# Sliding-window attention followed by a gated network: the first weight block is consumed by contraction halves, the third tile's output also takes seven products, and the order of the work is drawn up anew

## The chip, the cores and the metric

The kernel runs on one core of a Trainium2 chip. A core has a matrix engine (PE, whose weight loads are listed as PEld), a vector engine (DVE), a scalar engine (ACT), a general engine (POOL, which here also issues the loads from DRAM) and a synchronising engine (SP, which here issues the stores). PE multiplies a stationary block by a moving block and writes to one of eight accumulator banks of 128 partitions by 512 floats. The metric is the device time of one execution in microseconds (us).

## The reference

Attention over 8 batches, 8 heads, 576 positions and head size 64, where a position sees itself and the 63 before it; the result, as 4608 rows of 512, goes through a gated network of inner width 1536.

```python
scores = scale * np.matmul(q, k.transpose(0, 1, 3, 2))
rel = pos[:, None] - pos[None, :]
mask = (rel >= 0) & (rel < 64)
attn = softmax(np.where(mask, scores, -1e9))
x = (attn @ v).transpose(0, 2, 1, 3).reshape(4608, 512)
out = (np.maximum(x @ w_gate, 0.0) * (x @ w_val)) @ w_out
```

Inputs and output are float32 in DRAM; the kernel computes in 16-bit floats with float32 accumulation.

## The kernel before

**Tiles.** The 4608 rows are nine tiles of 512 rows, numbered 0 to 8. A tile is eight windows of 64 positions. For each tile the kernel computes scores (L377, L385), exponentials (ACT, L645), the product with v (L391), a reciprocal and a scaling into `xw` (DVE, L660 and L398), and a transpose into the stationary layout `xt` (DVE, `turn`, L403). Then come the two hidden products with the gate and the value weights, the rectifier and their product into `g_sb`, and the output product with `wo`.

**Two ways to multiply.** Tile 0's hidden layer is direct (`direct_block`, PE at L750, rectifier on ACT at L760, product on DVE at L762). The hidden layers of tiles 1 to 8 (`fast_hidden`, PE at L842) form the two-by-two block product by seven block products in place of eight: sums of weight blocks (`us`, `vs`, formed once at L791), sums of x blocks (L716), and sums of results (DVE, L858). The output is direct for the tiles below `TF` (`output`, PE at L916: 12 groups of four 512-column products for each tile) and by seven products from tile `TF` on (`fast_output`, PE at L1005: 14 groups of six 256-column products, four sums of `g_sb` blocks on DVE at L973, three sums of results on DVE at L1041). The latter needs sums of blocks of `wo` (`w_sums`, L950), one of which is written over `wo` itself, and so only after the last direct output.

**The start.** `first_part` is written out by hand. Tile 0's first six windows are two units of 192 rows (u = 0 and 1), each in two head halves (hh = 0 and 1) of 256 of the 512 columns of x. The list of steps is: 93 small products of zeros on PE (`PADS`, L424), loads of the first q, k and v, the first four of 12 column blocks of the gate weight `wg` and then of the value weight `wv`, each in two halves a = 0 and 1 of the contraction (`w_part`, L337), scores and values of both units, and for each unit and head half a `recip`, a `norm` and a `turn`. Products of zeros (`keep_hot`, L453, three times, and L502 into bank 7) lie between the steps on PE. The half a = 0 of the contraction is head half 0 of x, and a = 1 is head half 1.

**The rest.** `second_part` lists every other step as an `Op` with a key, an expected duration on each engine that can do it, the steps that it comes after, and the accumulator banks and buffers that it takes and gives back. `Plan.run` walks through expected time when the program is built. For each engine it takes the ready step with the lowest key, and it emits the steps in that order. So the order on each engine's queue is fixed by the keys, which come from the table `K` (one value for a kind of step, and a correction for each tile under `K["d"]`), by the expected durations, and by the times at which engines, banks and transfers are expected to be free after the first part. Loads are issued by POOL, in the order of their keys, between its arithmetic. `Plan.fetch` models the arrival of PE's own instructions; `Plan.fill` counts products into long waits, though `emit` leaves those out of the program.

**Tile 0, first two units.** `direct_block` is called for u = 0 and 1 and for two pairs of the first four 128-wide column blocks. Each call does, for each column block, the four contraction steps of one weight in a row:

```python
for b, f in enumerate(fs):
    for c in range(NC):
        nc.tensor.matmul(bank[i][:, b * n:b * n + n], wt[:, c, f * 128:f * 128 + 128],
                         xs[0][:, c, c0:c0 + n], start=(c == 0), stop=(c == NC - 1))
```

Of the kernel before, what the change touches and what calls it, by code (L numbers as in the profile page):

```python
# [12 lines left out]
ACT = mybir.ActivationFunctionType  # L13
MUL = mybir.AluOpType.mult
ADD = mybir.AluOpType.add
SUB = mybir.AluOpType.subtract
MAX = mybir.AluOpType.max
ONE_ONE = struct.unpack("<f", struct.pack("<I", 0x3C003C00))[0]


K = {"T1": 33.417, "STEP": 29.94, "wo1": 24.303, "wo2": 136.509, "q0": 0.81, "q1": 2.61, "q10": -9.561, "q11": 1.093, "v": -0.6, "v1": 1.142, "ql": 1.41, "qt": 0.88, "qti": 4.69, "vl": 0.91, "vc": 0.04, "vm": 1.83, "e": 7.62, "gap": 3.77, "gap1": -1.003, "r": -6.21, "tn": 1.66, "xf": 4.78, "wf": -1.338, "wfj": 2.6, "sn": 2.67, "su": -2.15, "re": 17.5, "mu": -6.61, "la": -4.79, "o0": 11.594, "o0j": 20.432, "o0s": -4.369, "oo": 0.007, "os": 0.386, "oj": 4.81, "gs": -1.18, "fo": 0.015, "fi": 0.098, "fs": 4.74, "fu": 0.27, "W0": 129.92, "TF": 3, "rs": 7.037, "rv": 3.751, "rt": 4.292, "wl": 1.63, "wln": 5.389, "l0": 0.003, "l1": 4.021, "lv": 1.186, "lvs": 12.368, "wo0": 25.921, "db": -7.955, "di": 1.563, "dv": 0.646, "slack": 0.3, "d2": 3.05, "bl": 9.0, "lv0": 18.364, "d": {'0:q0': 0.808, '0:fs': 1.88, '0:la': 1.692, '1:oo': 0.058, '0:fi': 0.024, '1:qt': 3.036, '1:os': -0.226, '0:vc': -1.15, '0:tn': -0.981, '0:qt': 0.904, '0:e': -2.629, '0:sn': 0.475, '0:vm': 0.58, '0:vl': 0.514, '0:ql': 0.128, '0:fu': -2.028, '1:tn': 3.174, '0:re': 0.858, '1:ql': -1.577, '0:xf': -0.14, '0:su': 0.053, '0:gap': 0.391, '0:r': -2.955, '0:oo': -0.042, '0:os': 0.025, '1:vm': 0.483, '1:fo': -0.017, '0:q1': 0.357, '1:sn': 0.632, '0:oj': -0.104, '0:qti': -0.947, '0:gs': -0.096, '0:fo': -0.029, '2:xf': -3.116, '1:oj': -0.851, '1:fu': -1.619, '1:gs': -1.956, '1:vl': 3.671, '1:fs': -1.692, '1:q0': -0.44, '1:re': 17.838, '1:qti': -0.251, '2:vl': -1.63, '1:xf': 0.54, '2:v': 0.897, '2:e': 3.091, '1:vc': -0.626, '2:gap': 1.519, '1:mu': -1.202, '2:oj': 1.272, '2:os': -0.152, '1:gap': -2.068, '1:su': 1.664, '1:q1': 0.09, '1:la': -0.927, '2:fu': -0.861, '2:q0': -1.678, '2:su': -3.121, '1:v': 0.703, '1:r': 0.099, '2:tn': 0.263, '2:mu': -0.767, '2:qti': -1.435, '2:sn': 0.235, '2:qt': 0.357, '3:re': -0.971, '3:su': 1.85, '2:gs': 0.316, '2:vc': -0.222, '2:fi': 0.018, '3:fs': 2.376, '2:oo': -0.024, '3:gs': -0.499, '2:ql': 2.087, '2:re': 1.781, '2:vm': -0.346, '2:la': -0.408, '3:fo': 0.105, '3:qt': -1.251, '3:qti': -0.756, '3:fi': 0.003, '3:r': 4.605, '4:tn': 4.441, '4:fo': 0.176, '3:sn': 1.86, '3:v': -0.191, '3:gap': 0.067, '3:q1': -1.861, '4:v': -2.381, '3:fu': -1.0, '3:e': -2.398, '3:ql': 0.244, '3:q0': -0.417, '4:ql': 1.859, '4:qti': -0.846, '3:oo': 0.017, '3:oj': -1.455, '3:mu': 5.549, '3:vl': -0.094, '3:la': -1.756, '3:os': 0.07, '4:qt': -2.162, '5:v': 2.345, '5:e': -6.12, '5:gap': -0.396, '4:re': 16.126, '4:r': -3.179, '4:os': 0.054, '4:q0': -0.903, '4:gap': -1.023, '4:fu': -1.144, '5:vm': 1.185, '4:fi': -0.029, '4:vm': 1.023, '4:la': 2.23, '4:vl': 0.037, '5:tn': -1.009, '5:r': -1.653, '5:fu': 0.073, '5:re': 3.794, '4:q1': 1.992, '4:sn': 1.164, '4:xf': -1.831, '5:fi': -0.019, '4:mu': 1.169, '4:oj': 1.089, '5:qti': -1.537, '5:fo': -0.021, '5:xf': -1.396, '5:gs': -0.82, '5:mu': -2.334, '5:vc': -0.566, '5:oo': 0.002, '5:q0': -0.047, '4:vc': 0.378, '5:qt': -1.506, '4:fs': 0.072, '5:ql': -0.361, '5:oj': 0.91, '5:fs': -0.532, '5:q1': -0.028, '4:oo': -0.002, '5:la': 0.275, '6:oo': -0.051, '6:vl': -1.345, '6:v': 0.087, '7:vc': 2.102, '6:os': 0.034, '7:fo': -0.026, '6:tn': -1.475, '6:gap': -1.442, '6:xf': 3.27, '6:fi': -0.035, '6:fo': -0.054, '6:fu': -0.179, '6:qt': 0.741, '7:tn': -0.289, '7:vl': -0.177, '6:ql': -0.604, '7:re': 9.431, '7:fi': 0.019, '7:xf': -0.992, '6:vc': -0.932, '7:sn': -0.018, '6:e': 6.905, '6:q1': 1.236, '7:ql': -0.482, '7:e': -4.862, '7:qt': 1.66, '6:mu': -0.73, '7:gap': 0.823, '6:oj': 0.303, '6:q0': 0.231, '6:r': 2.887, '7:su': 1.478, '7:gs': -0.403, '7:q0': -0.079, '7:q1': -0.303, '7:vm': -1.095, '6:gs': -0.02, '7:mu': -0.49, '7:fs': 1.309, '7:la': -0.048, '7:os': 0.117, '7:qti': -1.407, '7:r': -0.97, '7:fu': -0.866, '6:re': 0.021, '6:la': 0.896, '7:oo': -0.007, '6:sn': 0.915}}


PLANS = []


class Op:
# [16 lines left out]
class Plan:  # L44
# [70 lines left out]
    def fill(self, o, t, emit):  # L115
        if t - self.free["PE"] < 0.7:
            return
# [1006 lines left out]
```

## Time and profile before

| what | value |
|---|---|
| median of 3 runs | 308.0 us (307.89 to 308.69) |
| profiled execution, its own time | 309.13 us |
| span of the profiled execution | 307.2 us |
| DVE, ACT, POOL busy | 246.2, 213.0, 229.8 us |
| transfers on the loads' queue | 18.29 MB as written, 51.1% of 16 engines' span |
| hidden layers of tiles 1 to 8, PE L842 | 1344 products of 128x256 |
| direct outputs of tiles 0, 1, 2, PE L916 | 144 products of 128x512 |
| seven-product outputs of tiles 3 to 8, PE L1005 | 504 products of 128x256 in the program |

The span runs from the first to the last recorded instruction; the 1.93 us between it and the execution's own time lie around it. PE's busy time is from modelled ends: a 128x256 product is shown as 273 ns long though the next starts 109 ns later, so short pauses between products do not show as idle. A row of the timeline has start, duration, engine, line and operation, tiles, shapes, the number of instructions merged into it, and in brackets how long the engine sat idle before the first of them and what ended that. A row of windows has, for a stretch, its length, each engine's busy time in it with the number of instructions, PE's granted clock, the mean busy share of the 16 transfer engines (over 1 where packets overlap) and the rate in GB/s.

### The profile page before, as it was taken

Reading aid. Unit: us, or ns where it says so; the run is one execution under the profiler, and the core shown is the slowest. Engines: PE = TensorE matmul, PEld = TensorE weight load, DVE = VectorE, ACT = ScalarE, POOL = GpSimd, SP = SyncE. Lnnn points to the kernel's source line nnn. Section 1 sums busy time; section 2 is a strip of 40 time slices with the busy share of each in tenths; the row PEclk is TensorE's granted clock in tenths of the full one; section 3 lists DMA queues with packets and bytes.
Section 4 is the critical chain, followed back from the end, with each engine's and each line's share of the span. In section 5 each row is a group of like instructions: output and inputs, shape, how many; then the busy total and the mean of one; then the engine's idle time right before and its main releaser. Section 6 shows DMA issues by size and latency. Waiting matters only on the chain.

```text
span 307.2 us, 11254 instructions
## 1 busy us (share of the span) xinstructions
PE 297.1 (97%) x4772; PEld 240.2 (78%) x4772; DVE 246.2 (80%) x422; ACT 213.0 (69%) x414; POOL 229.8 (75%) x233
## 2 busy tenths in 40 slices
PE   7889999998999999999999999999999999999995
PEld 5475845786757886777888888888888888888884
DVE  5858997988963997887989988878896789595762
ACT  4445335897768787788778786778687886878721
POOL 8696957998999899999189954995479157938520
PEclk9999999999999999999999999999999999999999
DMA  7999999983249953996694194674112011201033
GB/s 219 187 190 206 196 194 198 202 169 22 19 78 150 183 99 75 139 182 136 123 72 82 34 165 120 48 166 37 54 36 69 6 38 37 68 0 36 1 121 120
DMA packets 59074, 32.87 MB, mean 107 GB/s; under 512 B 39440, under 2 KB 53392, under 8 KB 59024
## 3 DMA queue, kind: packets, MB, share of 16 engines
q0 software_dynamic: 46672, 18.29, 51.1%
q1 hardware_dynamic: 12208, 13.80, 14.2%
q8 instruction: 37, 0.61, 0.8%
q14 instruction: 13, 0.11, 0.1%
q10 hardware_dynamic: 144, 0.07, 0.1%
HBM read 37.75 MB, written 9.44 MB: 154 GB/s over the span
## 4 chain that ended last, share of the span: by engine, by line
PE 85%; DMA 8%; POOL 3%; issue 2%; DVE 1%; ACT 0%; ACTq 0%; DVEq 0%; POOLq 0%
PE bank L842 48%; PE bank L1005 18%; PE bank L916 8%; PE bank L391 4%; PE bank L750 3%; DMA wo<-in_moe_w_out_dram 3%; DMA wv<-in_moe_w_val_dram 3%; DMA k<-in_k_dram 2%; PE bank L385 2%; PE bank L377 1%; POOL vs L791 1%; POOL v L356 1%; POOL q L347 0%; POOL k L347 0%; DVE xw L398 0%
## 5 line engine op out<-in xcount | busy, mean ns | idle before, releaser
L876 POOL TENSOR_TENSOR g_sb<-pr,pr 128x512 f16<-128x512 f32 x96 | 121.6, 1283 | 47.7 <-ACT pr L889 16.5
L858 DVE TENSOR_TENSOR pr<-bank,pr 128x512 f32<-128x512 f32 x144 | 92.6, 678 | 24.7 <-PE bank L842 21.9
L851 ACT COPY pr<-bank 128x512 f32<-128x512 f32 x144 | 79.9, 590 | 30.2 <-PE bank L842 27.9
L842 PE MATMUL bank<-xt,vs 128*128 128x256 f16 x384 | 56.7, 273 | 0.0
L842 PE MATMUL bank<-xt,us 128*128 128x256 f16 x384 | 56.2, 273 | 0.0
L867 ACT ACTIVATE pr<-pr 128x512 f32<-128x512 f32 x72 | 45.4, 639 | 5.9 <-DVE pr L858 5.5
L842 PE MATMUL bank<-xt,wg 128*128 128x256 f16 x288 | 42.8, 273 | 0.0
L842 PE MATMUL bank<-xt,wv 128*128 128x256 f16 x288 | 42.7, 273 | 0.0
L842 PEld LDWEIGHTS <-us 128*128 128x128 f16 x384 | 37.0, 98 | 6.5 <-issue 0.2
L842 PEld LDWEIGHTS <-vs 128*128 128x128 f16 x384 | 37.2, 98 | 4.7
L645 ACT ACTIVATE p<-bank 128x512 f16<-128x512 f32 (+1 forms) x68 | 35.7, 592 | 6.7 <-PE bank L385 6.5
L916 PE MATMUL bank<-wo,g_sb 128*128 128x512 f16 x144 | 35.9, 380 | 0.3 <-DMA wo<-in_moe_w_out_dram 0.3
L356 POOL DMA_DIRECT2D v<-in_v_dram x40 | 34.9, 883 | 0.5 <-issue 0.5
L889 ACT ACTIVATE pr<-bank 128x512 f32<-128x512 f32 x48 | 27.1, 601 | 6.7 <-PE bank L842 5.0
L842 PEld LDWEIGHTS <-wg 128*128 128x128 f16 x288 | 27.7, 98 | 4.7
L842 PEld LDWEIGHTS <-wv 128*128 128x128 f16 x288 | 28.1, 98 | 4.2
L1005 PEld LDWEIGHTS <-g_sb 128*128 128x128 f16 x288 | 27.9, 98 | 3.4
L1005 PE MATMUL bank<-wo,g_sb 128*128 128x256 f16 x216 | 28.4, 273 | 0.0
L398 DVE TENSOR_TENSOR xw<-bank,r 128x448 f16<-128x448 f32 (+2 forms) x45 | 25.8, 575 | 1.5
L403 DVE STREAM_TRANSPOSE xt<-xw 128x512 f16<-128x512 f16 (+2 forms) x38 | 25.0, 668 | 0.5 <-ACT xw L506 0.3
L1005 PEld LDWEIGHTS <-ss 128*128 128x128 f16 x216 | 21.0, 98 | 2.5
L916 PEld LDWEIGHTS <-g_sb 128*128 128x128 f16 x144 | 13.5, 98 | 11.3 <-issue 0.3
(95 smaller groups left out, 389.4 us busy)
## 6 DMA issues: line engine op xcount, KB each, us to landing
out_dram<-pr SPq DMA_DIRECT2D x35, 256.0 KB, 2.4
k<-in_k_dram POOLq DMA_DIRECT2D x15, 288.0 KB, 7.5
q<-in_q_dram POOLq DMA_DIRECT2D x15, 288.0 KB, 7.1
v<-in_v_dram POOLq DMA_DIRECT2D x32, 128.0 KB, 6.4
v<-v SPq DMA_DIRECT2D x12, 132.0 KB, 2.6
v<-v SPq DMA_DIRECT2D x24, 66.0 KB, 2.3
wg<-in_moe_w_gate_dram POOLq DMA_DIRECT2D x6, 256.0 KB, 6.6
wv<-in_moe_w_val_dram POOLq DMA_DIRECT2D x6, 256.0 KB, 7.9
```

Of the source, the lines that this page charges most:

```text
L356: nc.gpsimd.dma_start(v16s[b % 2][lo:hi, g, :, 0:64], v[b, :, 64 * g - 64 + lo:64 * g - 64 + hi].rearrange("h p d -> p h d"))
L398: nc.vector.tensor_tensor(x, blocks_of(to, n)[:, :, 0:D].rearrange("p s (c e) -> p s e c", e=2), r[:, :, :, None].to_broadcast([128, n, 2, ...
L403: nc.vector.transpose(xt[:, 2 * hh:2 * hh + 2, c0:c0 + n].rearrange("p e (s c) -> p s e c", c=32), x)
L645: nc.scalar.activation(pp[g][:, 0:n].rearrange("p n c -> p (n c)"), st[g][:, 0:64 * n], ACT.Exp, scale=scale)
L842: nc.tensor.matmul(slot[to][:, HT * m:HT * m + HT], w[:, kk, 128 * m:128 * m + 128], x[:, kk], start=(first and m == 0 and kk == 0), stop= ...
L851: lambda e, hold=hold, slot=slot: nc.scalar.copy(hold["x"], slot["A"]),
L858: nc.vector.tensor_tensor(hold["x"], slot[to], hold["x"], ADD)
L867: lambda e: nc.scalar.activation(hold["x"], hold["x"], ACT.Relu), after=[o])
L876: lambda e: VEC[e].tensor_tensor(gh[:, fs:fs + 2, h], pair(a["x"]), pair(b["x"]), MUL),
L889: lambda e, hold=hold, slot=slot, i=i: nc.scalar.activation(hold["x"], slot["A"], ACT.Copy if i else ACT.Relu),
L916: nc.tensor.matmul(bank["b"][:, 0:c1 - c0], gs[t % 2][:, f, 128 * sub:128 * sub + 128], wo[:, f, c0:c1], start=(j == 0 and i == 0), stop=( ...
L1005: nc.tensor.matmul(bank[to][:, HD * m:HD * m + HD], a[:, f, 128 * m:128 * m + 128], b[:, f], start=(first and m == 0 and f == 0), stop=(f ...
```

## The change

In the first part: the loads of the first weight block go in the order gate a = 0, value a = 0, gate a = 1, value a = 1; before it was both of gate, then both of value. The second unit's values follow the first unit's directly on PE; a `keep_hot` and the product of zeros into bank 7 between them are gone, and 78 small products of zeros stand at the start in place of 93. On DVE, head half 0 of unit 0 is turned right after its own `norm`; head half 1 of unit 0 is turned after its `norm` and both of unit 1's reciprocals.

In tile 0's first two units, `direct_halves` takes the place of `direct_block`. Each weight's work on a pair of column blocks is two steps, one for each half of the contraction, and a list `SEQ` of (unit, gate or value, half) gives the order of the eight; each waits for its own half of x and of the weight. `mark` tells the plan at what time these halves are expected.

In the table: `TF` is 2 in place of 3, so that tile 2's output is formed by seven products and the sums of `wo` come after tile 1's direct output. All other keys are new, with corrections for tile 8 too; `fill` is gone, and a constant in the model of instruction arrival is 4.8 where 6.5 stood. Among the keys are those of the weight loads: `wl` is -2.164 (1.63), `wln` 11.938 (5.389), `wo0`, `wo1`, `wo2` are 23.517, 27.481, 29.198 (25.921, 24.303, 136.509), `l0`, `l1` are -1.828, 7.977 (0.003, 4.021), `lv`, `lvs` are 2.594, 2.169 (1.186, 12.368), `lv0` is 14.48 (18.364), and `T1` is 48.436 (33.417).

```diff
-K = {"T1": 33.417, ... "TF": 3, ...}
+K = {"T1": 48.436, ... "TF": 2, ... "pads": 78, "cap": 4.8}
...
-    PADS = 93
+    PADS = int(K["pads"])
...
-        for wt, src in ((wg, moe_w_gate), (wv, moe_w_val)):
-            for a in range(2):
+        for a in range(2):
+            for wt, src in ((wg, moe_w_gate), (wv, moe_w_val)):
                 w_part(wt, src, 0, 4, a)
...
-        keep_hot(banks[2][:, 0:2 * U])
         copies(1, nc.gpsimd.tensor_copy, 0, H)
+        for hh in range(2):
+            values(1, hh)
...
-        for hh in range(2):
-            recip(0, hh)
-            norm_of(0, hh)
-        for hh in range(2):
-            turn(xs[0], hh, 0, x_of(0, hh))
-        for hh in range(2):
-            values(1, hh)
-        nc.tensor.matmul(banks[7], zero[:, 0:128], zero, start=True, stop=True)
-        for hh in range(2):
+        recip(0, 0)
+        norm_of(0, 0)
+        turn(xs[0], 0, 0, x_of(0, 0))
+        recip(0, 1)
+        norm_of(0, 1)
+        for hh in (1, 0):
             recip(1, hh)
         for s in range(SB):
             nc.scalar.activation(x_of(1, 1)[:, s], ...)
+        turn(xs[0], 1, 0, x_of(0, 1))
         norm_of(1, 0)
         for hh in range(2):
             turn(xs[0], hh, U, x_of(1, hh))
...
+        SEQ = ((0, 0, 0), (0, 1, 0), (0, 0, 1), (U, 0, 0), (U, 1, 0), (0, 1, 1), (U, 0, 1), (U, 1, 1))
+        def direct_halves(c0, fs):
...
+            for place, (u, i, a) in enumerate(SEQ):
+                if u != c0:
+                    continue
+                def mm(e, wt=(wg, wv)[i], i=i, a=a):
+                    for b, f in enumerate(fs):
+                        for c in (2 * a, 2 * a + 1):
+                            nc.tensor.matmul(bank[i][:, b * U:b * U + U], wt[:, c, f * 128:f * 128 + 128], xs[0][:, c, c0:c0 + U],
+                                             start=(a == 0 and c == 0 and b == 0), stop=(c == NC - 1), skip_group_check=True)
+                after = [xa[c0, a]] + ([came[i, a]] if (i, a) in came else []) + ([ran[i, 0]] if a else [])
...
         for s in (0, U):
             for w in range(2):
-                direct_block((T0 - 2 + 0.6 * w + 2 * (s > 0), T0 + 1.5 + 0.6 * w + 0.1 * (s > 0)),
-                             range(2 * w, 2 * w + 2), s, U, x0[s])
+                direct_halves(s, range(2 * w, 2 * w + 2))
```

More of the change, by code (lines that the diff above doesn't have):

```diff
@@ L113, in fetch, with transfer @@
         return t
-    def fill(self, o, t, emit):
-        if t - self.free["PE"] < 0.7:
-            return
-        free = [(self.taken[id(h[n])], h[n]) for pool, h, names in o.take if "bank" in pool for n in names]
-        free += [(x[0], x[2]) for pool in ("bank", "bo") for x in self.pools[pool]]
-        if free or self.open:
-            since, bank = min(free, key=lambda x: x[0]) if free else (0.0, self.open[-1]["b"])
-            since = max(self.free["PE"], since + 0.1)
-            n = int((t - 0.25 - since) / 0.165)
-            if n > 0:
-                self.fetch(2 * n, since, 0.165 * n, True)
-                self.filled.append((since, n, t, o.name))
-                emit((bank, bool(free)), n)
+    def transfer(self, dma, t):
+        nbytes, rate, which = dma
+        self.queue[which] = max(self.queue[which], t + 1.2) + nbytes / rate
+        return self.queue[which] + 0.8
     def finish(self, o, e, t, dur):
@@ L143, in finish @@
         if o.dma:
[L144 to L146 removed]
+            end = self.transfer(o.dma, end)
             if e == "POOL":
@@ L765, in direct_block, with mark @@
                 gates.setdefault((0, f), []).append((c0, mul))
-        x0 = {0: [], U: [plan.op("", 0.0, {"DVE": (0.0, False)}, lambda e: None)]}
+        marks = []
+        def mark(t):
+            marks.append(op("", 0.0, {"SP": (t - 3.0 if not marks else t - marks[-1].when, False)}, lambda e: None, after=marks[-1:]))
+            marks[-1].when = t
+            return marks[-1]
+        xa, came = {}, {}
+        for to, key, t in ((xa, (0, 0), 14.3), (came, (1, 0), 14.9), (xa, (0, 1), 15.85), (came, (0, 1), 16.15), (xa, (U, 0), 16.95),
+                           (xa, (U, 1), 17.5), (came, (1, 1), 17.7)):
+            to[key] = mark(t)
```

48 lines of the change are left out of this document (27 added, 21 removed).

## The prediction

> **What bounds the kernel now.** First the page's head and busy rows. PE is the only engine near the span; an idle microsecond of DVE, ACT or POOL costs nothing as long as PE has work.
>
> ```profile
> span 307.2 us, 11254 instructions
> PE 297.1 (97%) x4772; PEld 240.2 (78%) x4772; DVE 246.2 (80%) x422; ACT 213.0 (69%) x414; POOL 229.8 (75%) x233
> ```
>
> Second the table of stretches. From 22 us on PE is idle for 0.24, 0.52, 1.20 and 0.31 us in the rows below and not at all between 80 and 143 or between 173 and 291, 2.27 us in all. There, PE work that is taken away shows as time. DVE and POOL are nearly full where tile 2's direct output runs (30.43 and 34.08 of 35 us), and have room where the first seven-product output runs (POOL 22.30 of 30).
>
> ```profile
> 22.00:40.00 18.00, 17.76 (x304) 12.77 (x296) 15.83 (x35) 7.79 (x16) 14.64 (x18) 1.00 1.36 200
> 40.00:52.00 12.00, 11.48 (x255) 5.65 (x243) 10.19 (x20) 5.35 (x10) 7.02 (x10) 1.00 1.38 200
> 52.00:80.00 28.00, 26.80 (x466) 21.58 (x465) 25.57 (x45) 22.48 (x44) 25.34 (x25) 1.00 0.82 119
> ...
> 108.00:143.00 35.00, 35.00 (x518) 26.36 (x516) 30.43 (x47) 27.18 (x52) 34.08 (x35) 1.00 0.85 126
> 143.00:173.00 30.00, 29.69 (x512) 25.91 (x511) 25.90 (x45) 24.38 (x46) 22.30 (x22) 1.00 0.59 83
> ```
>
> Third the timeline of the start. Tile 0's first products begin at 15.03, stop for 1.01 us for the last piece of the first value block, and hand over at 21.87.
>
> ```profile
> 13.33 0.91 PE L453 MATMUL bank<-zero 128*128 128x384 f32 x2
> 14.41 1.03 DVE L403 STREAM_TRANSPOSE xt<-xw 128x384 f16<-128x384 f16 x2
> 15.03 1.77 PE L750 MATMUL bank<-xt,wg 128*128 128x192 f16 x16
> 17.97 1.33 PE L750 MATMUL bank<-xt,wv 128*128 128x192 f16 x14 [1.01 <-DMA wv<-in_moe_w_val_dram]
> 21.87 0.29 PE L377 MATMUL bank<-ident,biasT 32*128 32x128 f16 x8
> ```
>
> Fourth the chain that ended last. Up to 50 us it passes through loads twice: the value block that lands at 17.93 and the third block of `wo` that lands at 50.09.
>
> ```profile
> 9.26 8.67 DMA wv<-in_moe_w_val_dram
> ...
> 41.17 8.92 DMA wo<-in_moe_w_out_dram
> 50.13 1.02 PE bank L916 x4
> ...
> 104.52 0.86 PE bank L916 x4
> ...
> 144.94 0.65 PE bank L1005 x6
> ```
>
> **The change, part by part. The start.** The work is 64 products of 192 columns, which start 83 ns apart in the trace: eight groups of 8, 0.66 us each. I place them by rows of before. Values of unit 1 need POOL's copies, which end at 13.68 (12.41 and 1.27); 0.56 us of values end near 14.2. Head half 0 is scaled by 13.80 and its turn, now right behind, takes 0.58: 14.4. The first four pieces of weight land at 13.60, 14.84, 16.12 and 17.93 in the trace; the second and third are swapped, so gate a = 0 keeps 13.60, value a = 0 has 14.84 and gate a = 1 has 16.12. DVE then does reciprocal and scaling of half 1 (0.18, 0.56), two reciprocals (0.23), turn (0.58), unit 1's scaling (0.56) and turns (0.58 each): half 1 is ready near 16.1, unit 1's halves near 17.2 and 17.8. Groups in the listed order then start at 14.4, 15.1, 16.15, 17.2, 17.85, 18.5, 19.2, 19.85 and end at 20.5. Against 21.87 that is 1.4 us. The turn that is moved behind four DVE steps costs nothing, since gate a = 1 lands at 16.12 anyway. If all waited for nothing from 15.07 on, the end would be near 19.7 and the gain 2.2; if unit 1 came as late as the gate's second piece can make it, by 1.28 us, the gain would be 0.1. I take 1.4, by the rows. POOL issues the same four loads in another order, at no cost.
>
> The products of zeros that go (0.91 and 0.39 us) filled waits for POOL and DVE; without them PE idles there instead, less by what the next steps move up, which is counted above. The 15 small products at 28 ns (0.4 us) end before the wait of 0.5 us for `bias` that follows: nothing.
>
> **Tile 2's output.** In the chain a group of the direct form takes 0.86 us and one of the seven-product form 0.65 to 0.66: 12 x 0.86 = 10.32 less 14 x 0.655 = 9.17 is 1.15 us of PE, in a stretch where PE never idles. DVE gets four sums (0.95, 0.96, 1.11, 0.95: 3.97 us) and three sums of results (0.68 each: 2.04), 6.0 us in all; ACT gives four copies for three and one, the same; SP's stores stay four.
>
> ```profile
> L1041 DVE TENSOR_TENSOR pr<-bank,pr 128x512 f32<-128x512 f32 x18 | 12.2, 680 | 4.7 <-PE bank L1005 4.6
> L973 DVE TENSOR_TENSOR g_sb<-g_sb 128x1536 f16<-128x1536 f16 x5 | 5.6, 1110 | 0.0
> L716 DVE TENSOR_TENSOR xt<-xt,xt 128x512 f16<-128x512 f16 x7 | 7.7, 1101 | 0.7
> ```
>
> What hides the 6.0: DVE idles 4.57 of 35 us in the row 108 to 143, and the sums come when tile 2's hidden layer ends, so part falls behind it. Bounds: nothing, and 4.0 us if POOL too stands still for the four sums and PE for POOL. The last group above suggests that DVE and POOL exclude each other: the same sum of 512 takes 417 ns in one execution and 1101 on the mean here. That fits the Trainium skill, "SBUF — State Buffer", section "Who interferes with whom": the two share a port pair under an exclusive lock; by it alone the sum would be 4.0 us worse. The nearest row is 143 to 173, where the first seven-product output's sums ran and PE lost 0.31 us, most of it elsewhere than at its products; I take 0. The sums of `wo` are the same twelve, of which eight already ran at 55 to 70 us on POOL; only the in-place ones (0.40 us x 3 on DVE at 143.29) move up.
>
> **The loads.** By the keys POOL's order from 13.6 us becomes gate blocks 2 and 1, the last v of batch 0, value block 2, k and q of batch 1 (head half 0), `wo`, value block 1, v, `wo`, v, `wo`, k and q (half 1). Landing steps in the trace: 1.3 us for a piece of weight, 1.4 for k or q, 2.6 for a `wo`, 0.9 for a v. Value block 2 lands by 26.48, k and q by 29.25, `wo` by 31.85, value block 1 by 34.45 (29.07 for both blocks before). PE from 20.5: scores 0.4, two gate blocks 5.3, values 0.4, value block 2 2.6, the third unit's 80 products of 128 columns 4.5, scores of tile 1 0.7, that is 34.4. So it just fits. Then the last `wo` lands near 42.4 in place of 50.09, and k and q of half 1 near 45.3 in place of 42.99; with two turns (1.24 each) tile 1's second scores can start at 47.8, against 46.42 before, while PE arrives earlier. Only batch 2's k and q (2.8 us) were removed from ahead of the `wo`. A stall between 0 and 2.8 us (1.4 later and 1.4 earlier) stands here; direct output and tile 1's first-half products cover most, so I take 0.4.
>
> **The rest of the order.** Bounds: all 2.27 us of idle goes, or each of seven later tiles has a stop like the worst single one, 1.03 us at 70.5 (PE at L391 waiting for nothing visible), 7.2 less 2.27: 4.9 worse. Both orders come from the same rule, and before shows 0.31 in 210 us: I take 0.
>
> **Sum.** -1.4 - 1.15 + 0.4 = -2.15. The profiled execution took 309.13 (span 307.2, 1.93 around it) and would take 307.0; it stands 1.1 above the median of the runs. On the median: 308.0 - 2.15 = 305.8 us.
>
> **Rivals.** (1) The transfers eat the start: PE arrives early and waits for k and q of half 1. For it: about 200 GB/s in both rows up to 52 us. Against: PE idles only 0.76 us there, and the last `wo` comes sooner. With the stall at 1.4 to 2.8 in place of 0.4 the time is 306.9 to 308.2; the front part then does nothing.
>
> (2) Slower: the four sums of tile 2 hold POOL in the stretch where it has 0.92 us spare in 35, its products into `g_sb` come late, and PE, ACT and the banks wait for them. Price up to 4.0: 309.4 with the other terms at -1.4 - 1.15 and no other stall. It decides if more than 3.5 of the 4.0 reach PE. Against: 143 to 173.
>
> (3) Slower: the new order is looser, by up to 4.9: 310.7, half of it 308.3.
>
> (4) PE's own clock. The eight 128x384 products at L448 start 320 ns apart, those at L750 with 384 columns 163, though the granted clock reads 1.00: PE runs at half rate up to about 7.5 us. With 15 fewer products ahead full rate could come one stretch later; the two products L453 (0.64 each) and first scores then take 1.3 us longer, of which DVE's wait at 11.39 hides nothing in the worst case: 307.1. The Trainium skill, "TensorE: Matmul & The Clock Gate", part 1, says that activity in a free-running window of about 3.4 us releases the clock and an idle window throttles it; here the longest new pause is under 1 us, so by that rule too only the start is at risk.
>
> (5) Better: the idle goes too, 303.5.
>
> **How the numbers follow.** Chances: forecast 0.52 (304.0 to 307.0, from the start's gain between 1.0 and 2.2 and the order within 1 us), (1) 0.16, (2) 0.13, (3) 0.09, (4) 0.05, (5) 0.05. A measurement can tell about 0.3%, 0.92 us. Faster, under 307.08: forecast, (5), half of (1): 0.65. Same: the other half and (4): 0.13. Slower, over 308.92: (2) and (3): 0.22. The range leaves out (5) and most of (3): 303.9 to 309.6.
>
> **What would show it.** Start right: the eight groups begin near 14.4 and PE takes up the third unit's scores near 20.5. Loads right: value block 1 lands near 34.4, the last `wo` near 42.4, and PE's idle up to 55 us stays under 1.2. Output right: 96 products left at the direct output's line, 588 at the other, tile 2's sums inside a stretch where PE stays full. Wrong if PE idles over 2 us in a stretch between 50 and 145, or if the start's gain is found again as a wait at tile 1.

## The result, and the profile after

| | before | after |
|---|---|---|
| median | 307.94 us (307.54 to 308.69, 6 runs) | 315.42 us (315.12 to 316.74, 6 runs) |
| ratio, 95% interval | | 1.0245 (1.0222 to 1.0267) |
| profiled execution: own time, span | 309.13, 307.2 us | 315.42, 313.6 us |
| mean granted clock of the profiled execution | 0.999 | 0.984 |

The change makes the kernel 7.5 us slower, where 2.2 us faster was forecast. The time is outside the range (303.9 to 309.6) and on the other side. Here and below, ratios and their intervals leave out executions that took over 1.5% more than the fastest of the same kernel.

The head, the busy rows and the clock row of the page of after, the clock row in 40 slices of 7.8 us:

```profile
span 313.6 us, 11291 instructions
PE 298.3 (95%) x4790; PEld 245.5 (78%) x4790; DVE 253.4 (81%) x429; ACT 213.8 (68%) x416; POOL 227.4 (73%) x231
...
PEclk9899999797999999999999999999999999999999
```

PE shows 1.2 us more busy time in a span that is 6.4 us longer; the clock row dips around 8 to 16 us and twice between 55 and 78.

The table of stretches of after, with the same bounds as before's:

```profile
22.00:40.00 18.00, 17.57 (x262) 12.33 (x261) 15.40 (x38) 9.73 (x20) 14.54 (x18) 1.00 1.45 197
40.00:52.00 12.00, 12.00 (x182) 5.88 (x179) 11.23 (x18) 5.60 (x11) 8.70 (x10) 1.00 1.23 200
52.00:80.00 28.00, 21.65 (x465) 16.50 (x465) 17.86 (x33) 16.52 (x32) 16.31 (x18) 0.88 0.96 133
...
108.00:143.00 35.00, 35.00 (x557) 30.08 (x556) 30.84 (x50) 26.96 (x51) 28.02 (x27) 1.00 0.71 105
143.00:173.00 30.00, 29.66 (x513) 25.83 (x511) 27.26 (x46) 23.64 (x45) 25.73 (x25) 1.00 0.77 115
```

One row holds the loss. In 52 to 80 PE is idle for 6.35 us (28.00 less 21.65) where it was 1.20, and the granted clock there is 0.88 where it was 1.00. In the other rows shown PE's idle time is as before, within 0.03 us, or less.

The start, in the timeline of after:

```profile
15.05 1.44 PE L779 MATMUL bank<-xt,wg 128*128 128x192 f16 x8 [0.35 <-DVE xt L387]
16.28 1.25 PE L779 MATMUL bank<-xt,wv 128*128 128x192 f16 x8
17.36 1.48 PE L779 MATMUL bank<-xt,wg 128*128 128x192 f16 x16
...
20.66 0.82 PE L779 MATMUL bank<-xt,wv 128*128 128x192 f16 x8
21.42 0.29 PE L361 MATMUL bank<-ident,biasT 32*128 32x128 f16 x8
```

Tile 0's first units hand over at 21.42, only 0.45 earlier than before's 21.87. The first two groups take 1.23 and 1.08 us from start to start (16.28 less 15.05, 17.36 less 16.28), the last one 0.76: the first ran at half rate.

The chain that ended last, in order of time, in the stretch of the loss:

```profile
52.07 0.46 PE bank L375 x33
...
56.14 0.72 PE bank L867 x5
56.86 1.64 issue
58.50 4.57 PE bank L867 x28
63.08 7.31 DMA v<-v
70.43 0.28 PE bank L375 x10
```

Before, the chain passed through the first value block and the third `wo`; now it passes through neither, but through the copies of v within the core's own memory (`v<-v`, issued by SP at L602). That PE releases the copy at 63.08 is the profile's inference; the copy is issued right behind the landing of the second v load (62.99), and experiment 1 shows the same copy at the same time with PE further on. PE's timeline at that place:

```profile
56.59 0.27 PE L867 MATMUL bank<-xt,wv 128*128 128x256 f16 x1
58.50 0.80 PE L867 MATMUL bank<-xt,wv 128*128 128x256 f16 x3 [1.64 <-issue]
59.09 1.91 PE L867 MATMUL bank<-xt,us 128*128 128x256 f16 x8
60.80 1.39 PE L867 MATMUL bank<-xt,vs 128*128 128x256 f16 x8
...
66.49 0.30 PE L375 MATMUL bank<-v,p 128*32 128x65 f16 x16
70.43 0.28 PE L375 MATMUL bank<-v,p 128*32 128x65 f16 x12 [3.64 <-DMA v<-v]
70.64 0.61 PE L867 MATMUL bank<-xt,vs 128*128 128x256 f16 x4
```

PE stops for 1.64 us in the middle of a group, and for 3.64 us in the values of tile 2 (L375), until the first copy of batch 2's v has landed (70.39). Tile 1's hidden products stand right behind (70.64 and on), but the order on PE's queue is fixed. The eight products at 59.09 take 1.71 us until the next group starts at 60.80, eight from 64.21 take 0.87 until 65.08: half rate again.

**The clock.** The table of stretches, with bounds set at the changes of the granted clock:

```profile
10.31:13.72 3.41, 1.83 (x90) 1.06 (x89) 3.11 (x6) 2.57 (x13) 1.32 (x3) 1.00 1.51 197
13.72:17.13 3.41, 3.04 (x70) 2.87 (x70) 3.27 (x10) 1.59 (x8) 3.41 (x5) 0.50 1.20 197
54.69:58.10 3.41, 1.51 (x11) 0.82 (x10) 2.98 (x7) 3.10 (x7) 3.19 (x4) 1.00 1.06 207
58.10:61.51 3.41, 3.01 (x15) 2.08 (x15) 2.10 (x4) 0.84 (x2) 1.93 (x3) 0.50 2.11 172
...
64.92:68.33 3.41, 1.87 (x32) 1.42 (x30) 1.81 (x3) 2.76 (x6) 1.61 (x2) 1.00 1.02 170
68.33:71.75 3.42, 1.32 (x23) 1.15 (x23) 0.89 (x3) 0.00 (x0) 0.92 (x1) 1.00 0.71 181
71.75:75.16 3.41, 3.41 (x109) 2.46 (x107) 2.52 (x4) 2.56 (x5) 1.41 (x2) 0.50 0.11 11
```

Three stretches of 3.41 us ran at half rate, each right behind one in which PE was busy for 1.83, 1.51 and 1.32 us (54, 44 and 39%). In before's corresponding stretch at the start, 9.80 to 13.21 by steps of 3.41 us back from the one change of its clock at 306.8, PE was busy for 2.35 us (69%), and the clock stayed at 1.00. But the stretch from 64.92, with 1.87 us (55%), was followed by one at full rate, so the busy share alone does not tell when the clock falls.

**The account** of PE's time, by these rows: 5.15 us more idle in 52 to 80; two half-rate stretches there, whose 3.01 and 3.41 us of busy time would have been half as long (3.2); less 1.15 for tile 2's products, 0.45 for the handover and 0.33 for less idle in 22 to 52; plus 0.17 of idle behind 143. That is 6.6 us; the spans differ by 6.4. (The medians differ by 7.5, since before's profiled execution stood 1.2 above its median.) The account adds up PE's time and is no list of causes: experiment 1 shows that the stop of 1.64 us and the first of the two late half-rate stretches (1.5 us) fall into time in which PE would have waited for v anyway.

**Why v is late.** Landings in the two traces, in us:

| step | before | after |
|---|---|---|
| third block of `wo` lands | 50.09 | 42.39 |
| k, q of batch 1, half 1, land | 40.08, 42.99 | 43.90, 45.37 |
| PE starts tile 1's second scores | 46.42 | 48.69 |
| first v load of batch 2 is issued, lands | 49.35, 55.14 | 52.40, 62.16 |
| stores of tile 0 issued just then | 51.80, 53.32 | 51.99, 52.48, 52.97 |
| first copy of v is issued, lands | 56.06, 60.25 | 63.08, 70.39 |
| q, k, q of batch 3 are issued | 58.98, 61.93, 62.53 | 61.80, 62.42, 62.97 |

The first copy lands 10.14 us later: 3.05 because the loads are issued later (batch 2's v goes into batch 0's buffer, and the last values that read it are tile 1's, behind its second scores; they start at 49.30 before and at 52.00 after, and in after POOL is busy issuing a load of k up to 52.40); 3.97 because a load takes 9.76 us in place of 5.79; 3.12 between the load's landing and the copy's (8.23 in place of 5.11), all of it in the copy itself (7.31 in place of 4.19). The direct output of tile 0, which before was spread until `wo` had come, runs in one block to 52, so three of its four stores of 256 KB are issued within one microsecond, around the first v load. The transfers that were issued between 50 and 62, of after:

```profile
out_dram<-pr SPq DMA_DIRECT2D x3, 256.0 KB, 8.1
v<-in_v_dram POOLq DMA_DIRECT2D x4, 128.0 KB, 9.7
```

Over the whole run a store lands in 2.4 us and a v load in 6.0 on the median. That the loads and stores collide was at this point a reading of two traces. The experiments test it.

### The profile page after: what moved, and what is told of

Its sections match the earlier page's. It is cut to its first block, busy times and chain, and to the rows that moved or that the text cites. A ratio compares the mean times of both kernels' runs of the same rounds, so it can differ in the third digit from the quotient of the medians.

```text
span 313.6 us, 11291 instructions
## 1 busy us (share of the span) xinstructions
PE 298.3 (95%) x4790; PEld 245.5 (78%) x4790; DVE 253.4 (81%) x429; ACT 213.8 (68%) x416; POOL 227.4 (73%) x231
## 4 chain that ended last, share of the span: by engine, by line
PE 89%; DMA 4%; DVE 2%; issue 2%; POOL 1%; ACT 1%; ACTq 0%; DVEq 0%; POOLq 0%
PE bank L867 46%; PE bank L1030 21%; PE bank L941 7%; PE bank L732 5%; PE bank L375 4%; PE bank L369 3%; DMA v<-v 2%; DMA v<-in_v_dram 2%; PE bank L779 2%; PE bank L361 2%; DVE v L456 1%; DVE xw L382 1%; DVE xt L387 0%; POOL v L340 0%; POOL k L331 0%
## 5 line engine op out<-in xcount | busy, mean ns | idle before, releaser
L883 DVE TENSOR_TENSOR pr<-bank,pr 128x512 f32<-128x512 f32 x144 | 92.8, 681 | 24.5 <-PE bank L867 17.9
L867 PE MATMUL bank<-xt,us 128*128 128x256 f16 x384 | 57.1, 276 | 0.0
L1030 PEld LDWEIGHTS <-g_sb 128*128 128x128 f16 x336 | 32.6, 98 | 3.9
L1030 PE MATMUL bank<-wo,g_sb 128*128 128x256 f16 x252 | 33.1, 273 | 0.0
L1030 PEld LDWEIGHTS <-ss 128*128 128x128 f16 x252 | 24.4, 98 | 3.0
L941 PE MATMUL bank<-wo,g_sb 128*128 128x512 f16 x96 | 23.2, 379 | 0.0
L698 POOL TENSOR_TENSOR xt<-xt 128x512 f16<-128x512 f16 x16 | 18.6, 1159 | 5.8 <-DVE xt L387 3.8
```

What stands on the lines that cost most here:

```text
L867: nc.tensor.matmul(slot[to][:, HT * m:HT * m + HT], w[:, kk, 128 * m:128 * m + 128], x[:, kk], start=(first and m == 0 and kk == 0), stop= ...
L883: nc.vector.tensor_tensor(hold["x"], slot[to], hold["x"], ADD)
L941: nc.tensor.matmul(bank["b"][:, 0:c1 - c0], gs[t % 2][:, f, 128 * sub:128 * sub + 128], wo[:, f, c0:c1], start=(j == 0 and i == 0), stop=( ...
L1030: nc.tensor.matmul(bank[to][:, HD * m:HD * m + HD], a[:, f, 128 * m:128 * m + 128], b[:, f], start=(first and m == 0 and f == 0), stop=(f ...
```

## The experiments

Theory A: the transfers around batch 2's v (the three stores beside its loads, the loads of batch 3 behind them) make it late; it is a matter of order. Theory B: the products of zeros that were taken out of the start let the granted clock fall, and that is the loss. Theory C: the seven-product output of tile 2 costs more than it saves. Theory D: the new start in itself is slow. Each runs against before on the same chip.

**1. The two products of zeros put back into after.**

```diff
+        keep_hot(banks[2][:, 0:2 * U])
         copies(1, nc.gpsimd.tensor_copy, 0, H)
         for hh in range(2):
             values(1, hh)
+        nc.tensor.matmul(banks[7], zero[:, 0:128], zero, start=True, stop=True)
```

> The changed kernel with the two products of zeros (L453 and L502 of before) put back where they stood; everything else, the order of all later steps too, is the changed kernel's. If the loss comes from the throttled stretch at 13.7 to 17.1 us that the removed products let in, the granted clock reads 1.00 there, the eight groups of tile 0 start 83 ns apart per product, and the time falls by 0.7 to 1.4 us, to 314.0 to 314.7. If the loss is at the second tile's v (3.64 us of PE waiting for v at 66.8 and two throttled stretches at 58 and 72), most of the 7.5 us stays: no less than 313.5. If the throttle depends on the stretch before the products (10.3 to 13.7, PE about half busy) the throttle stays although they are back, and the time is 315 to 316.

Measured: 315.50 us (315.11 to 316.52), ratio 1.0251 (1.0230 to 1.0272). PE's timeline around 57 and at tile 2's values:

```profile
56.78 0.60 PE L869 MATMUL bank<-xt,wv 128*128 128x256 f16 x4
57.21 1.04 PE L869 MATMUL bank<-xt,us 128*128 128x256 f16 x8
...
63.42 0.30 PE L375 MATMUL bank<-v,p 128*32 128x65 f16 x16
70.34 0.36 PE L375 MATMUL bank<-v,p 128*32 128x65 f16 x12 [6.61 <-DMA v<-v]
```

The clock still fell, at 11.70 to 15.12 and at 66.32 to 73.14, and v was late. B falls as the cause of the loss, for these two products; the 15 small ones were not put back. The run shows more. The stop of 1.64 us is not there, though the same three stores are issued (52.18 to 53.16), and no half-rate stretch comes at 58. PE is at tile 2's values 3.07 us sooner (63.42 for 66.49) and waits 2.97 us longer; the first copy lands at 70.29 (70.39 in after), and the time is the same. So the stop and the first late half-rate stretch cost nothing beside the wait for v.

**2. The same two products taken out of before.**

```diff
-        keep_hot(banks[2][:, 0:2 * U])
         copies(1, nc.gpsimd.tensor_copy, 0, H)
...
-        nc.tensor.matmul(banks[7], zero[:, 0:128], zero, start=True, stop=True)
```

> The kernel before without the same two products of zeros, nothing else changed. If they are what keeps the clock up, a throttled stretch appears between 13 and 17 us, and the time rises by 0.5 to 1.7 us (308.5 to 309.7). If they only fill waits, the time stays within 0.5 us of 307.9 and the clock at 1.00.

Measured: 308.14 us (307.58 to 308.76), ratio 1.0003 (0.9991 to 1.0015). In six of ten executions the clock is 0.992 to 0.994, in four 1.000, and the medians are 308.4 and 308.1. So in before's order a half-rate stretch in the start does come (14.50 to 17.92 in the profile) and goes with no more than 0.3 us: PE hands over at 21.82, where it was 21.87, because in before it waits for the value block until 17.9 anyway.

**3. Three loads moved.** In after's order, with no duration touched, q, k and q of batch 3 go behind one later product of POOL (`mult`, step 224).

```diff
-        end = plan.run(emit)
+        steps = []
+        end = plan.run(lambda o, e: steps.append((o, e)))
+        late = [x for x in steps if x[0].name == "qk_load" and x[0].n in (526, 528, 530)]
+        steps = [x for x in steps if x not in late]
+        at = next(i for i, x in enumerate(steps) if x[0].name == "mult" and x[0].n == 224)
+        steps[at + 1:at + 1] = late
+        for o, e in steps:
+            emit(o, e)
```

> The changed kernel with three loads (q, k, q of batch 3, issued at 61.8 to 63.0 us) moved behind the second following product on POOL, about 5 us later; all other steps keep their order on every queue. If the v copies of batch 2 (7.3 us from issue to landing) are slow because these loads share the transfer engines, they land by 67 in place of 70.4, PE's wait of 3.64 us for v falls below 1 us, the throttled stretch at 71.8 goes, and the time falls by 3 to 5.5 us, to 310 to 312.5. If they are slow for the v loads still under way or for themselves, the landing moves by less than 1 us and the time by less than 1.5.

Measured: 310.08 us (309.37 to 310.73), ratio 1.0069 (1.0049 to 1.0090): 5.3 us of the 7.5 are back. The row of 52 to 80, and PE's timeline at tile 2's values:

```profile
52.00:80.00 28.00, 24.91 (x520) 20.29 (x520) 23.76 (x45) 21.54 (x42) 21.93 (x23) 1.00 0.97 134
```

```profile
65.71 0.28 PE L375 MATMUL bank<-v,p 128*32 128x65 f16 x12 [0.41 <-DMA v<-v]
```

The v loads land as late as in after (62.41), but the first copy takes 2.5 us (63.15 to 65.67) where it took 7.3. PE waits 0.41 us for 3.64, and neither late half-rate stretch comes. The stop of 1.64 us is still there. The first copy lands 4.72 us sooner (65.67 for 70.39), and PE goes on 4.72 sooner; the half-rate stretch behind 71.75, which does not come, was 1.7. That is 6.4, the same as wait and clock (3.2 + 3.2) by the account above; the span is 5.5 shorter, since 0.8 of new idle shows in 22 to 40 and 143 to 173. That the stretch at 58 is missing is not the work of loads that were issued behind it: the bounds lie elsewhere in this execution, and behind 56.80 to 60.21, with PE busy for 1.80 us (53%), the clock stays at 1.00.

**4. The three bunched stores left out of after** (rows 128 to 511 of tile 0).

```diff
+        steps = [x for x in steps if not (x[0].name == "store" and x[0].n in (133, 138, 143))]
```

> The changed kernel without three stores of tile 0 (rows 128 to 511 of the output, 768 KB, issued at 52.0 to 53.0 us): those rows are not written. If the v loads of batch 2 land 3 to 4 us late because these stores share the transfer engines, they land near 58 to 60 in place of 62 to 64, the v copies 3 us sooner, PE's stop of 1.64 us inside a group at 56.9 shrinks if it is a late block of instructions, and the time falls by 3 to 6 us, to 309.5 to 312.5. If the cause is the late issue alone (52.4 against 49.35 before), the time falls by less than 1.5.

Measured: median 310.2 us, from 306.47 to 313.89 in six executions; ratio 1.0085 (1.0064 to 1.0106), without the two longest. The profiled execution is the fastest of them (306.47). In it the first three v loads land at 57.2 to 58.9, the first two copies at 61.2 and 61.4, the stop of 1.64 us is gone, the clock does not fall, and 52 to 80 reads

```profile
52.00:80.00 28.00, 26.93 (x492) 21.77 (x481) 26.01 (x47) 22.66 (x44) 24.35 (x25) 1.00 0.83 102
```

So the stores do delay the loads: the first takes 5.4 us from issue to landing, where it took 9.8. That they cause the stop is not shown, since experiment 1 has them and no stop. What the slower executions lost is not known: only one was profiled.

**5. Stores moved too, then one load of k.** On top of 3: the three stores go behind the fourth copy of v on SP; and on top of that, k of batch 3 goes behind batch 2's third v load.

```diff
+        held = [x for x in steps if x[0].name == "store" and x[0].n in (133, 138, 143)]
+        steps = [x for x in steps if x not in held]
+        at = next(i for i, x in enumerate(steps) if x[0].name == "v_move" and x[0].n == 340)
+        steps[at + 1:at + 1] = held
...
+        load = next(x for x in steps if x[0].name == "qk_load" and x[0].n == 524)
+        steps.remove(load)
+        at = next(i for i, x in enumerate(steps) if x[0].name == "v_load" and x[0].n == 338)
+        steps.insert(at + 1, load)
```

> The changed kernel with the three loads of batch 3 moved behind as in the run before, and the three stores of tile 0 moved on SP behind the first four v copies of batch 2; nothing is left out and PE, ACT and DVE keep their order. If stores and loads together make v late, the v loads land by 59 as they did without the stores, PE's stop inside a group near 57 is gone, PE's idle time from 52 to 80 us falls from 3.1 to about 1.5, and the time is 306.5 to 308.5, 1.5 to 3.5 below the run with the loads moved alone. If the held stores keep buffers that ACT then waits for, or if the rest of the new order is looser by itself, the time stays above 309.

> The same, and the load of k of batch 3 that stands ahead of batch 2's v loads on POOL goes behind the third of them. If v is still late with the stores moved, this brings it 1.4 us sooner and 0.3 to 1.5 us of time; if v is no longer on the path, the time is that of the run without this move within 0.5 us.

Measured: 309.28 us, ratio 1.0034 (1.0010 to 1.0057), and 308.52, ratio 1.0014 (0.9995 to 1.0033), 12 executions each. With k moved the v loads land at 54.9 to 57.4, as early as in before. What is late next, in the second one's waits of PE:

```profile
PE bank L867 <- ACT pr L876: 1.3, 2, 1.0
```

The held stores keep their buffers, so ACT waits to write tile 1's next results and PE waits for ACT. Theory A holds: seven transfers moved, without a change to any product, take the kernel from 315.4 to 308.5. The late issue of the v loads needed no mending for that: in the first of these two runs they go out at 51.97, 2.6 us later than in before, and PE does not wait for v.

**6. The new start alone, in before's order.** Weight order, values and turns of the first units and the eight half groups as in the change; all else as before.

```diff
-        for wt, src in ((wg, moe_w_gate), (wv, moe_w_val)):
-            for a in range(2):
+        for a in range(2):
+            for wt, src in ((wg, moe_w_gate), (wv, moe_w_val)):
                 w_part(wt, src, 0, 4, a)
...
+        turn(xs[0], 0, 0, x_of(0, 0))
+        recip(0, 1)
...
+                ops[-1].half = lambda a, wt=wt, i=i: half(wt, i, a)
```

> The kernel before with the start of the changed kernel alone: the order of the first four weight loads, unit 1's values without the two products of zeros, the turns for each head half and the eight half-contraction groups; 93 small products and the old order of all later steps are kept. If the start's gain reaches the end, PE takes up the third unit's scores at 20.5 to 21.2 in place of 21.87 and the time falls by 0.7 to 1.4 us, to 306.6 to 307.3. If PE merely waits longer for the later loads (the third block of wo lands at 50.09, whatever PE does), PE's idle time from 22 to 52 us grows by as much and the time stays within 0.5 us of 308.

Measured: 307.75 us (306.56 to 310.05, 12 executions), ratio 0.9981 (0.9952 to 1.0010). In the profile, at clock 1.00:

```profile
14.39 0.82 PE L756 MATMUL bank<-xt,wg 128*128 128x192 f16 x8 [0.23 <-DVE xt L404]
15.05 0.82 PE L756 MATMUL bank<-xt,wv 128*128 128x192 f16 x8
16.09 1.49 PE L756 MATMUL bank<-xt,wg 128*128 128x192 f16 x16 [0.22 <-DVE xw L399]
...
20.16 0.29 PE L378 MATMUL bank<-ident,biasT 32*128 32x128 f16 x8
```

```profile
22.00:40.00 18.00, 16.84 (x260) 11.80 (x259) 16.54 (x36) 7.71 (x16) 16.27 (x21) 1.00 1.39 200
40.00:52.00 12.00, 11.11 (x239) 5.55 (x238) 9.52 (x20) 4.24 (x8) 6.11 (x9) 1.00 1.37 199
```

The handover is 1.7 us earlier than before's, and PE then idles 2.05 us in 22 to 52 where it idled 0.76: it waits for weights' sums (0.7), `wo` (0.7), a transpose of x (0.4) and exponentials (0.2). Three quarters of the gain (1.29 of 1.71) is waited away by 52. The profiled span is 1.5 us shorter than before's all the same, as the idle time in 52 to 80 is 1.05 less; but that execution of before stood above its median, and the medians differ by 0.4. So D falls, and so does most of the start's gain.

**7. The third tile's output alone.** In before, only `TF` goes from 3 to 2; the order is then drawn anew from the old keys.

```diff
-K = {"T1": 33.417, ... "TF": 3, ...}
+K = {"T1": 33.417, ... "TF": 2, ...}
```

> The kernel before with one number changed: TF is 2 in place of 3, so that tile 2's output takes seven products; keys and start are the old ones. The order is the old one up to 108 us on every queue and is drawn up anew from there. If the saved 1.15 us of PE work is what counts, the time is 306.4 to 307.3. If the old keys no longer fit the steps that follow, PE idles in the stretches after 108 us and the time is 309 or more; the difference then measures the order, not the seven products.

Measured: 315.54 us (313.97 to 316.92, 4 executions), ratio 1.0237 (1.0193 to 1.0281). The rows from 108 on, and PE's longest waits:

```profile
108.00:143.00 35.00, 32.80 (x533) 27.58 (x531) 33.23 (x50) 26.16 (x50) 32.38 (x33) 1.00 0.75 103
143.00:173.00 30.00, 28.05 (x496) 24.07 (x494) 25.62 (x43) 22.27 (x42) 25.31 (x25) 1.00 0.76 111
173.00:291.00 118.00, 115.67 (x1767) 100.89 (x1765) 90.18 (x145) 87.15 (x164) 75.75 (x66) 0.99 0.28 57
```

```profile
PE bank L842 <- issue: 2.3, 1, 2.3
PE bank L1005 <- issue: 2.0, 1, 2.0
PE bank L842 <- POOL xt L716: 1.5, 1, 1.5
```

Here the loss lies behind 108 and not at 52 to 80. With the old keys the form loses 7.4 us; in after, with keys of its own, PE is full from 80 to 143. The products cost no time in one order and much in the other, so C is not decided by this run, but it falls by after's rows. The run does show what the prediction left out: one line of the table re-draws every later order, at a price of several microseconds.

**8. Can the new start be made to pay?** On experiment 6: q of batch 2 behind the third `wo`; then also products of zeros in PE's waits between 10 and 14 us (a narrow `keep_hot` behind the first scores and three zero products around the first unit's values).

```diff
+        load = next(x for x in steps if isinstance(x[0], Op) and x[0].n == 314)
+        steps.remove(load)
+        at = next(i for i, x in enumerate(steps) if isinstance(x[0], Op) and x[0].n == 11)
+        steps.insert(at + 1, load)
...
+                keep_hot(st[0][0][:, 0:128])
...
+            for _ in range(2 - hh):
+                nc.tensor.matmul(banks[2], zero[:, 0:128], zero, start=True, stop=True)
```

> The kernel before with the start alone, as run before, and one load (q of batch 2, half 0) moved behind the third block of wo on POOL. If the start's gain was lost to later loads, the third wo lands 1.4 us sooner (48.3 in place of 49.75), PE's wait of 0.65 us for it goes and the time falls by 0.4 to 0.8 us, to 306.9 to 307.4; if it was lost elsewhere (PE's 0.68 us at 39.5 for the sums of weights, slower clock in some executions), the time stays within 0.3 us of 307.75.

> The same, with small products of zeros put where PE waits between 10 and 14 us: one float product of 128 columns behind the first half's scores, and three of 512 columns behind unit 0's values. If the executions near 309 to 310 of the start alone are those with a throttled start (three of twelve read 0.994 and took 308.95, 308.95 and 310.05, the other nine 306.56 to 308.57), they go, all executions read 0.998 or more, and the median falls by 0.1 to 0.5 us; if the fillers themselves hold up values, it rises by 0.2 to 0.8.

Measured: 308.05 and 307.85 us, ratios 0.9985 (0.9960 to 1.0010) and 1.0001 (0.9964 to 1.0037). In the first the wait for `wo` is gone and idle in 22 to 52 falls from 2.05 to 0.95 us, yet the time is the same; one of its 12 executions took 603.55 us, which nothing here explains. In the second, the start again with those products, four executions still took 311 to 313 us at clocks of 0.988 to 0.993. Neither helped.

**9. The corrected after.** On top of experiment 5: one store is let go early, so that no buffer is held long; then the products of zeros of experiment 8 as well.

```diff
-        held = [x for x in steps if x[0].name == "store" and x[0].n in (133, 138, 143)]
+        held = [x for x in steps if x[0].name == "store" and x[0].n in (133, 138)]
```

> The changed kernel with the loads moved as in the run with k behind, and only two of the three stores moved behind the v copies, the first left where it was, since ACT waited 1.21 us for its buffer. That wait and PE's 1.0 us behind it go: 307.3 to 308.2 in place of 308.5. If the one early store holds the v loads up again, PE waits for v and the time is above 308.5.

> The same with the small products of zeros as in the other kernel. Seven of twelve executions of the run with k behind read 0.994 or less; if a throttled start costs time once the later waits are gone, the median falls by 0.3 to 1.0 us against the run without them; if the start is hidden behind loads, it stays within 0.3 us.

Measured: 308.17 us, ratio 0.9994 (0.9973 to 1.0016), and 307.80, ratio 0.9982 (0.9960 to 1.0004), 12 executions each. The second is the best version found. The row of 52 to 80:

```profile
52.00:80.00 28.00, 26.81 (x480) 21.53 (x472) 25.82 (x47) 22.38 (x44) 23.94 (x26) 1.00 0.89 131
```

Here idle is 1.19 us, as in before (1.20), and all 12 executions have a clock of 0.997 or more. In the one without these products six of 12 had a lower clock, and both halves have a median of 308.1 to 308.2, so the fall of the clock in the start cost nothing that can be told there. The interval of the best version reaches from 1.2 us faster to no change: the measurement does not separate it from before.

## Why the prediction was wrong, point by point

**The start: its working right at full clock, its cover wrong.** In experiment 6, at full clock, the groups begin at 14.39, 15.05 and 16.09, for 14.4, 15.1 and 16.15 worked out, and hand over at 20.16, for 20.5. In after they hand over at 21.42, 1.26 us later: 0.66 lies ahead of the first group (DVE's turn of head half 0 starts at 14.42 for 13.76), 0.6 in the first two groups, at half rate. Rival (4) has this size, 1.3, but not this mechanism. It feared that full rate would come one stretch later; the early products start as in before (4.74 and 7.27 us, for 4.75 and 7.28), and the clock fell again behind 13.72. That the sizes agree is luck. (The 1.00 that rival (4) reads for the first microseconds is no record: the trace's records of the clock begin at 9.80.) The products of zeros that go were said to fill waits and so to cost nothing. Whether they held the clock up is half answered: without two of them in before's order six of ten executions read 0.994 or less, where 2 of 35 of before did; put back into after, they did not keep it from falling.

**The loads: landings right, the step behind them missing.** Value block 1 was placed at 34.45, the last `wo` at 42.4, k and q of half 1 at 45.3 and the second scores at 47.8. They came at 35.13, 42.39, 45.37 and 48.69, and idle up to 55 us is 0.84 us (0.43 in 22 to 52, 0.41 at 53.48), under the 1.2 given. (By the landing steps that the working lists, the last `wo` comes out near 41.45; that 42.4 was met to 0.01 is in part luck.) The step was priced at 0.4, up to 2.8 at most, and that is right as far as tile 1's scores. It ended there. The working asked what PE waits for at that place, but not what the 2.3 us that the scores come later move: the last reading of batch 0's v, hence the v loads of batch 2, hence the copies on SP, hence tile 2's values on PE. The queue of SP was passed over too: the direct output, which no longer waits for `wo`, puts out three stores in 1 us, beside the first of these loads, and the loads of batch 3 run beside the copies.

**"The rest of the order: 0" failed, and it holds the loss.** Two bounds were worked out, 4.9 worse and 2.27 better. The loss in 52 to 80 is 8.4 us (5.15 idle, 3.2 clock), more than the worse bound, because that bound took the largest stop that before shows (1.03) as the size of a stop in an order that before does not show. Rival (3), the looser order, had 9% and the right sign; its price was too small by 3.5 us. The sign that was named for it, PE idle for over 2 us in a stretch between 50 and 145, did come (6.35).

**Rival (1)** happened in kind in experiment 6: the gain of the start is mostly waited away, though for weights' sums and `wo` and not for k and q. In after it did not, as argued: the last `wo` comes 7.7 us sooner.

**Rival (2)** did not happen. POOL is busy for 28.02 of 35 us in 108 to 143, and PE is full from 80 to 143.

**Tile 2's output** kept its place: 96 products at the direct line, 588 at the other, and PE full where the sums run. That PE's work is lower by 1.15 us is worked out; that the time falls by as much was not seen in any run.

**The clock** was counted as a matter of the start alone, as "the longest new pause is under 1 us". It fell again at 58.10 and 71.75, behind stretches with pauses of 1.64 and 3.64 us.

**Settled:** the loss is the late v of batch 2, with the half-rate stretch that follows the wait, and moving transfers alone removes it (315.4 to 308.5 and 308.2). **Open:** why the corrected order gains at most 1.2 us, where the start and tile 2's output together were worth 2.55; why the same products of zeros went with steady clocks in experiment 9 and not in 8; what decides when the clock falls; what makes the stop at 57; and what made the executions of experiment 4 spread. The 1.7 us for the half-rate stretch behind the wait is worked out from busy time; no run took it alone away.

## What to carry to other kernels

When a change moves loads, follow the buffer as well as the data: ask when the last reader of the old contents ends, which load that releases, what stands on the same queues at that time, and which engine takes the result in a fixed order. A change that re-draws an order cannot be priced by its parts or by the largest stop of the old order; put a range of several per cent on it, or look at the transfers around each change of batch. When an engine stops although work stands behind the waiting step, look at its transfers first: moving three loads here was worth 5.3 us, the whole corrected change at most 1.2. And a stop that lies ahead of a longer wait costs nothing by itself: here 1.64 us of stop and 1.5 us of slow clock came and went without moving the time.

## What the runs showed of the hardware

- **The clock can fall without an idle stretch, and the share of busy time alone does not say when.** Stretches of 3.41 us in which PE was busy for 54, 44 and 39% were each followed by one at half rate. The Trainium skill, "TensorE: Matmul & The Clock Gate", Part 1, says that the clock is throttled after an idle window of about 3.4 us and warns of idle gaps longer than that. The length of the stretch agrees with the trace. The warning covers the third fall, behind the pause of 3.64 us, but not the first two, with pauses of 0.77 and 1.64 us at most. A bound on the busy share does not sort them either: a stretch at 55% in after (64.92 to 68.33) and one at 53% in experiment 3 (56.80 to 60.21) were followed by full rate, one at 65% in experiment 2 (11.09 to 14.50) by half. What else decides is open. The bounds lie differently from execution to execution (at 9.80 in before's profile, at 10.31 in after's), and executions of one kernel differ: in experiment 2 six of ten had a lower clock and four had not.
- **Stores slow the loads beside them.** With three stores of 256 KB issued in 1 us, the first v load of 128 KB took 9.8 us to land; without the stores it took 5.4, with the stores moved behind (experiment 5) 5.9. The first copy of v within the core's memory took 2.5 us with no loads issued beside it and 7.3 with three.
- **PE can stop in the middle of a group while it waits for nothing that the profile shows.** In after and in experiment 3 it stood for 1.64 and 1.61 us from 56.86 on. A 16 KB packet on the instruction queue landed just then, at 57.18 and 57.15, after 1.49 and 2.37 us, where the next ones took 0.88 and 0.94; in experiment 1, with the same stores, it had landed at 54.82, and PE did not stop. The Trainium skill, "Runtime: NRT & Kernel Launch", section "Instruction fetch mechanics", calls crossing such a block mostly hidden. By these times it may not have been hidden where it came late. That the block caused the stop is read from the times and was not tried by itself; PE went on 1.3 us behind its landing.
